# Making the keys of a first softmax bound block by block, and queueing matmul products when their operand is done

## The chip, the cores and the metric

The kernel runs on one core of a Trainium2 chip. The metric is the device time of one execution in microseconds (us). The engines of a core work side by side, each through its own queue in order: PE (TensorE, matrix products), ACT (ScalarE, activation functions), DVE (VectorE), POOL (GpSimd) and SP (SyncE, which here issues nearly all transfers). An instruction that waits for an operand holds up all that is queued behind it on its engine.

## The reference

The input x has 2048 rows of 512 numbers. The result mixes self-attention with 32 heads of 16 numbers and a gated feed-forward network:

```python
g = sigmoid((x * gate_w).sum(-1, keepdims=True))
qkv = x @ wqkv                                   # 3 x 32 heads x 16
p = softmax(einsum("bhqd,bhkd->bhqk", q, k) / 4) # 2048 x 2048 for each head
a = einsum("bhqk,bhkd->bhqd", p, v) @ wo
b = (silu(x @ w_gate) * (x @ w_up)) @ w_down     # inner width 1792
return g * a + (1 - g) * b
```

All inputs and the output are bfloat16. The exponentials of 32 x 2048 x 2048 scores are most of the work outside the matrix products.

## The kernel before, in words

**Units, tiles and pairs.** A unit is one block of 512 queries for four heads: 4 x 8 = 32 units. The first four units are the first four heads for the four query blocks. A unit has 16 key tiles of 128 keys. A tile's scores are four products of 128 keys by 512 queries, one for each head. They come as two pairs: a pair fills a tile of two PSUM banks (`s_t`), and ACT makes its exponentials in one instruction of 128x1024 (`e_t<-s_t`). For some tiles, the V tiles, DVE makes the exponentials instead: PE writes single scores (`d_t`), DVE turns each into the bits of an approximate exponential, and two or three further passes over the whole tile, of which POOL may take a strip, refine it into two or four copies (`c_t`). V tiles are taken from the end of a unit's keys, tiles for ACT from its beginning. PE then multiplies either kind of numerator by the values (`o_ps<-e_t,vaug` and `o_ps<-c_t,vaug`); a V tile needs two or four such products, an ACT tile one.

**The bound.** The softmax does not look for a row's maximum. A bound on the scores, from a weighted sum of the magnitudes of q, goes into an extra row of the q operand. For the first four heads the weights are the largest magnitudes of k over all keys. At the start only 768 rows of x (`FK`, six key tiles, `FT`) have been loaded. So the kernel first makes a provisional bound from the keys of those rows (`kneg1`) and begins with the scores of the first six tiles with a q (`q0a`) that has this bound. Meanwhile the keys of the other 1280 rows are made in three blocks of 512, 512 and 256 (`k0_pieces`): four groups of matmuls each, `kp<-xT,mt` in the profile. DVE takes a block's largest magnitudes (`largest`, `kpart<-kp`) and copies the keys to SBUF (`kaug<-kp,onescol`). When the three blocks are done, `bound_all` folds their magnitudes into `kneg0` with three `k_neg` operations (`mt<-mt,kpart`). `q0_again` then has PE add the exact bound to a fresh q (`bound_add`, in the profile `qp<-mt`); `variants` copies this to SBUF and makes its two masked forms (`mt<-qp`, `qx<-mt,vsel`). Scores from the seventh tile on read this q, and so do all V tiles of the first unit. The part of the output that came from the first six tiles is later multiplied by the ratio of the two bounds.

**The order.** The order of every engine's instructions is written out when the kernel is built, by a planner. It keeps a clock for each engine (`plan.pe`, `plan.act`, `plan.dve`, `plan.pool`; 0 is the first pair's start), emits pairs, and fills what PE has left between them with value products and pieces of side work. Side work is in chains (`Chain`): a chain has a first slot (a slot is a tile's turn), a deadline, and chains that must have been emitted (`begun`) or finished (`after`) before. `pick` takes the ready chain with the earliest deadline; a chain with a deadline below 0 goes ahead of the one in progress. So in the kernel before, the fresh q's products (released at slot 1) are left after three of four pieces for the keys (slot 2). `later` queues DVE work with a cost and the time from which it can run; `need` forces a chain out at a given slot. PSUM has three banks for side work and `d_t`; ten numerator tiles can be open (`EB`).

**The marks.** `TURNS` is a string that steers the planner: of the two characters for pair n, the first concerns PE's filling, the second DVE's and POOL's choices, and "." leaves both to the standing rules.

Of the kernel before, what the change touches and what calls it, by code (L numbers as in the profile page):

```python
# [17 lines left out]
class Chain:  # L18
# [3 lines left out]
    def __init__(self, pieces, release, deadline, after=(), gap=0, cond=None, begun=()):  # L22
        self.begun = list(begun)
        self.pieces = list(pieces)
        self.n = len(self.pieces)
        self.rest = sum(p[0] for p in self.pieces)
        self.i = 0
        self.owed = 0
        self.release = release
        self.deadline = deadline  # L30
        self.after = list(after)
        self.gap = gap
        self.cond = cond
        self.done_at = None

    def out(self):
        return self.i >= self.n
# [4 lines left out]
    def ready(self, slot):  # L42
        if slot < self.release:
            return False
        for a in self.begun:
            if a.i < a.n:
                return False
        for a in self.after:
            if a.i < a.n or a.owed or slot < a.done_at + self.gap:
                return False  # L50
        return self.cond is None or self.cond()


class Pacer:
# [30 lines left out]


TURNS = (
    "........s...................k................w....o........l......a.b.........j.k.............a."
    "b............................x...............u...........l.................................q...."
    "...........v.n...uatf..tc..f............j.......a..............ya..........w.................ti."  # L90
    ".....m..f......t...l......c...s...i..lk.........b.........s.....k....v........e..u.............."
    "...q....................k..f............hx......................................e.......d......."
    ".....t.........v..............a....d.v.........f..jn.....r.................l..............d..g.."
    "s...k........x..c.j..nc...f...........h....gc.......h..v............a....x....e........f........"
    ".....m.u.q......................ow.................lh..........n.......g........c..v.......y...."
    "...ng.i...f..f........o.....................c............w..................j....n............o."
    "......................a......d...................l....i.......ex.......y........a.h...........h."
    "....f..........t...............m............j.................f.a...a........w.............f...."
    "..................a..........l.............mcq.r.........v.............w........................"
    "..............g..........................y.r.q..a.........d.............s.o....o..o.d..o...q...."  # L100
    ".......d............................................o........d.u....bt..e...j..f..s............."
    "..............................a.................e.....................h....n...dc..............."
    ".q.f......o....gh.........o...gn....o....d................d"
)


# [1 line left out]
def kernel(  # L108
# [400 lines left out]
    def k_bound(b):  # L509
        vec.tensor_reduce(out=kb[:, b:b + 1], in_=kst[b][:, :], axis=AX.X, op=ALU.max, apply_absolute_value=True)  # L510

    def v0(p, t0, i0, i1):

        for i in range(i0, i1):
            for dc in range(DC):
                mm(p[:, 64 * i:64 * i + 64], lhsT=xT[:, dc, (t0 + i) * P:(t0 + i + 1) * P], rhs=wv[:, dc, 0:64],
                   start=(dc == 0), stop=(dc == DC - 1))
# [5 lines left out]
    def v0_pieces(t0, n):  # L523

        st = {}

        def pc(k):
            def f():
                if k == 0:
                    st["p"] = m_tile("vp")  # L530
                for i in (k,):
                    for dc in range(DC):
                        mm(st["p"][:, 64 * i:64 * i + 64], lhsT=xT[:, dc, (t0 + i) * P:(t0 + i + 1) * P],
                           rhs=wv[:, dc, 0:64], start=(dc == 0), stop=(dc == DC - 1))
                spend("F", 0.8)
                if k == n - 1:
                    later(0.6, end)
            return f

        def end():  # L540
            vec.tensor_copy(**v0_out(st["p"], t0, n))
            m_free(st["p"], plan.dve)
        return [(0.8, pc(k), k == 0, "F", None) for k in range(n)]

    def v_pieces(tt):

        def end(p):
            dst = vaug[:, tt, 4 * VC:G * 4 * VC].rearrange("p (h c) -> p h c", c=VC)[:, :, 1:1 + DH]
            vec.tensor_scalar(out=ge[:, tt:tt + 1], in0=p[:, 63:64], scalar1=-40.0, scalar2=40.0, op0=ALU.max, op1=ALU.min)
            vec.tensor_copy(out=dst, in_=p[:, 64:D].rearrange("p (h c) -> p h c", c=DH))  # L550
            m_free(p, plan.dve)
        return columns(DC, "vp", lambda dc: xT[:, dc, tt * P:(tt + 1) * P], lambda dc: wv[:, dc, 63:D],
                       lambda p: later(0.69, lambda: end(p)), c0=63)

# [49 lines left out]
    def q0_pieces(qb):  # L604
# [11 lines left out]
        def clear():  # L616
            vec.tensor_scalar(out=mt[:, 5, :].bitcast(U16), in0=mt[:, 5, :].bitcast(U16), scalar1=0x7FFF, scalar2=None,
                              op0=ALU.bitwise_and)

        def bound():  # L620
            bound_add(st["p"], kneg0, mt[:, 5, :])
            spend("C", 1)
            variants(st["p"], q0[qb], work.tile([P, QBW], BF16, tag="qst", name="qst")[:, :])
        return (columns(DC, "qp", lambda dc: wpad[0][:, dc, :], lambda dc: xT[:, dc, qb * QBW:(qb + 1) * QBW], landed),
                [(1, bound, False)])

    def bound_add(p, kn, aq):
        for j in range(4):
            mm(p[32 * j:32 * j + 32, :], lhsT=kn[:, 32 * j:32 * j + 32], rhs=aq, start=False, stop=True,
               tile_position=(0, 32 * j), skip_group_check=True)  # L630

    def variants(p, to, q, more=()):

        def copy():
            vec.tensor_copy(out=q, in_=p[:, :])
# [2 lines left out]
        def select():  # L638
            for v in range(2):
                vec.tensor_scalar(out=to[:, v, :], in0=q, scalar1=vsel[:, v:v + 1], scalar2=None, op0=ALU.mult)  # L640
        key = object()
        later(0.6, copy, key=key)
        later(0.4, select, key=key)
# [109 lines left out]
    def emit_pair(bs, ride=0):  # L753
        i = pairs[0] % 2
        plan.pe = max(plan.pe + (FLIP if plan.mode != "R" else 0.0), s_end[i])
        plan.mode = "R"
        ride = d_slots(1 - bs[0] % 4 // 2)[:ride]
        s_t = ps_s.tile([P, 2 * QBW], F32, tag="s", name="s_t")
# [311 lines left out]
    def pv(n, k=None, most=QBW):  # L1070
# [9 lines left out]
            o_of[un] = ps_o.tile([P, QBW], F32, tag="o", name="o_ps")  # L1080
        if v_of(n) is not None:
            force(v_of(n))
        o = o_of[un]
        first = pvs[un] in ((0, FT) if un == 0 else (0,))
        last = un == 0 and pvs[un] == FT - 1 or pv_left(un) == 1
# [249 lines left out]
    def k0_pieces(i, k0, w):  # L1335
        c0 = QBW - w

        def end(p):
            def evict():
                vec.tensor_scalar(out=kaug[:, 0, k0:k0 + w], in0=p[:, c0:QBW], scalar1=onescol[:, 0:1],  # L1340
                                  scalar2=None, op0=ALU.add)
                m_free(p, plan.dve)
            later(0.67 if w == QBW else 0.4, lambda: largest(i, p[:, c0:QBW]))
            later(0.6 if w == QBW else 0.35, evict)
        return columns(DC, "kp", lambda dc: wpad[1][:, dc, :], lambda dc: xT[:, dc, k0:k0 + w], end, c0)

    def bound_all():
        def f():
            k_neg(kneg0, 2, kneg1)
            for i in (3, 4):  # L1350
                k_neg(kneg0, i, kneg0)
        later(1.1, f)

    again_ps = []

    def q0_again():
# [7 lines left out]
            ratio_done.append(plan.act + 0.1)  # L1364
        p = again_ps[0]
        bound_add(p, kneg0, aq0)
        spend("C", 1)
        variants(p, q0[0], q0_bf[1])
        at.setdefault(8, []).append(lambda: later(0.6, differ))
        at.setdefault(10, []).append(scale)  # L1370

    def scale_part(p):
        def f():
# [2 lines left out]
            part_scaled.append(0)  # L1376
        later(0.6, f)

    second = [pace.add(k0_pieces(2 + i, k0, min(QBW, S - k0)), 2, -100 + 0.1 * i)
              for i, k0 in enumerate(range(FK, S, QBW))]  # L1380
    known = pace.add([(0.2, bound_all, False)], 2, -98, second)
    qp_again = pace.add(columns(DC, "qp", lambda dc: wpad[0][:, dc, :], lambda dc: xT[:, dc, 0:QBW], again_ps.append),
                        1, -101)
    again = pace.add([(1, q0_again, False)], 2, -97, [known, qp_again])
    v_next = pace.add(v0_pieces(FT, 8), 2, -96)
    v_late = pace.add(v0_pieces(FT + 8, KT - FT - 8), 2, -95, [v_next])
    parts = pace.add(columns(1, "rp", lambda k: sbc_t, lambda k: ratio, scale_part), 3, 11, [again], 1,
                     cond=lambda: part_done and ratio_done and ratio_done[0] <= plan.pe)
    need[5] = [again]
    need[8] = [v_next]  # L1390
    need[10] = [v_late]
    need[14] = [parts]
# [8 lines left out]

        return v_rest[n - QB * KT] if QB * KT <= n < QB * KT + KT else None

    def v_done(n):
        return v_of(n) is None or v_of(n).done()
    prev = []
    for qb in range(1, QB):
        d = qb * KT
        q, bd = q0_pieces(qb)
        q = pace.add(q, 0, d - 13, [known])  # L1410
        bd = pace.add(bd, 0, d - 11, [q])
        need.setdefault(d - 5, []).append(bd)
        q_of[qb] = bd
    for qb in range(QB):
# [118 lines left out]
    def pv_list(now):  # L1533
# [7 lines left out]
        r = []  # L1541
        for n in range(un * KT + done_a[un], FT if early else un * KT + hi[un]):
            bs = range(4 * n, 4 * n + 4)
            if not all(b in e_end for b in bs) or now is not None and (max(e_end[b] for b in bs) > now or not v_done(n)):
                break
            r.append(n)
        r = [(n,) for n in r]
        r = r if early else [(n, k) for ready, n, k in vready if n // KT == un and (now is None or ready <= now and v_done(n))] + r
        item = cut.get("item")
        return r if item is None else [item] + [i for i in r if i != item]  # L1550

# [304 lines left out]
```

## Time and profile before

| what | value |
|---|---|
| median of three runs | 749.05 us (747.89 to 749.58) |
| the profiled execution's own time | 747.7 us |
| its span, first to last instruction | 746.0 us |
| mean granted PE clock | 0.998 of full speed |
| PE, ACT and DVE busy | 725.8, 729.8 and 719.5 us |
| numerator pairs on ACT | 756 |
| scores evicted by DVE for V tiles | 536, four to a tile |

The profile is of one execution. Times of single instructions are from the start of its span. A row of the list of instructions has the start, the time it took, the engine and line, the operation, what it writes and reads with shapes, and how many instructions are merged in it; in brackets the idle time before it and what ended that. Line 192 is the helper through which every matmul goes, 195 that of ACT and 204 that of DVE, POOL and SP, so operations are told apart by the tiles that they write and read. A row of the table by stretch has, for each engine, busy microseconds and in brackets the number of instructions, then the granted PE clock (1.00 is full speed), the mean busy share of the 16 DMA engines (it can exceed 1 where packets overlap) and the rate in GB/s. Weight loads (PEld) run beside the matmuls.

### The profile page before, as it was taken

What the parts mean: (1) busy time and instruction counts of PE and PEld (TensorE: products, weight loads), DVE (VectorE), ACT (ScalarE), POOL (GpSimd) and SP (SyncE); (2) the same over time, 40 slices, a digit from 0 to 9 for tenths busy, and PEclk for the clock granted to TensorE, in tenths of its full rate; (3) what the DMA queues carried; (4) which work ended last, traced back from release to release, by engine and by line L of the source; (5) the groups of instructions that cost most, each with busy time, mean ns of one, the idle gap of its engine ahead of it and who ended that gap; (6) DMA issues with size and microseconds to landing.
All of it is one profiled execution on the core that took longest, in us unless ns stands there. A gap on an engine that the chain in (4) does not pass through costs nothing.

```text
span 746.0 us, 22982 instructions
## 1 busy us (share of the span) xinstructions
PE 725.8 (97%) x9246; PEld 216.3 (29%) x9247; DVE 719.5 (96%) x1249; ACT 729.8 (98%) x828; POOL 289.6 (39%) x365
## 2 busy tenths in 40 slices
PE   8899999999999999999999999999999999999997
PEld 4222222223322222222222233322222332222222
DVE  5799999999999999999999999999999999999995
ACT  6899999999999999999999999999999999999996
POOL 7114244324442332444444345643344433454220
PEclk9999999999999999999999999999999999999999
DMA  9000212244120013211100132211000232100001
GB/s 224 10 2 16 52 30 44 58 118 117 37 52 13 13 28 96 62 42 32 42 19 10 43 87 46 68 36 41 20 13 26 63 82 56 34 20 13 16 30 36
DMA packets 91283, 34.45 MB, mean 46 GB/s; under 512 B 76000, under 2 KB 90728, under 8 KB 91176
## 3 DMA queue, kind: packets, MB, share of 16 engines
q1 hardware_dynamic: 89448, 32.66, 18.2%
q8 instruction: 72, 1.18, 0.6%
q10 hardware_dynamic: 1728, 0.33, 0.2%
q14 instruction: 35, 0.29, 0.1%
HBM read 21.42 MB, written 2.35 MB: 32 GB/s over the span
## 4 chain that ended last, share of the span: by engine, by line
PE 36%; DVE 14%; ACT 13%; issue 5%; DMA 0%; SPq 0%; DVEq 0%; ACTq 0%
PE s_t L192 12%; ACT e_t L195 12%; PE o_ps L192 11%; DVE c_t L204 10%; PE ops L192 7%; PE gu L192 4%; DVE kaug L204 1%; ACT th L195 1%; DVE mt L204 1%; DVE gs L204 1%; PE qp L192 1%; DMA on<-osb 0%; DVE osb L204 0%; DVE qst L204 0%; SPq L204 0%
## 5 line engine op out<-in xcount | busy, mean ns | idle before, releaser
L195 ACT ACTIVATE e_t<-s_t 128x1024 bf16<-128x1024 f32 x756 | 706.8, 1096 | 4.2 <-PE s_t L192 3.2
L204 DVE TENSOR_SCALAR c_t<-d_t 128x512 uint16<-128x512 f32 x456 | 300.2, 685 | 6.3 <-PE d_t L192 5.8
L192 PE MATMUL s_t<-qx,kaug 32*128 32x512 bf16 (+1 forms) x1200 | 234.0, 385 | 8.8 <-ACT e_t L195 7.0
L204 POOL TENSOR_SCALAR c_t<-c_t 128x352 uint16<-128x352 uint16 (+17 forms) x169 | 121.8, 720 | 189.1 <-DVE c_t L204 116.5
L192 PEld LDWEIGHTS <-kaug 32*128 32x128 bf16 (+1 forms) x2048 | 81.9, 91 | 308.5 <-issue 304.9
L192 PE MATMUL d_t<-qx,kaug 32*128 32x512 bf16 x440 | 151.2, 384 | 0.9 <-DVE qx L204 0.9
L192 PE MATMUL o_ps<-e_t,vaug 128*32 128x512 bf16 (+2 forms) x1600 | 150.2, 374 | 0.3 <-DVE vaug L204 0.3
L192 PE MATMUL o_ps<-c_t,vaug 128*32 128x512 bf16 (+2 forms) x1408 | 125.3, 371 | 0.1
L204 DVE TENSOR_SCALAR c_t<-c_t 128x2048 uint16<-128x2048 uint16 (+3 forms) x195 | 123.1, 646 | 0.6 <-PE o_ps L192 0.3
L204 POOL TENSOR_TENSOR c_t<-c_t 128x480 bf16<-128x480 bf16 (+9 forms) x58 | 65.6, 1145 | 130.8 <-DVE c_t L204 110.6
L192 PEld LDWEIGHTS <-vaug 128*32 128x32 bf16 x3232 | 68.0, 95 | 103.5 <-issue 89.5
L192 PE MATMUL gu<-xT,wg 128*32 128x512 bf16 x896 | 71.8, 383 | 0.0
L192 PE MATMUL gu<-xT,wu 128*32 128x512 bf16 x896 | 68.3, 382 | 0.4 <-DVE c_t L204 0.4
L192 PE MATMUL ops<-wd_t,mt 128*32 128x512 bf16 x672 | 56.8, 382 | 0.0
L204 DVE TENSOR_TENSOR c_t<-c_t 128x1568 bf16<-128x1568 bf16 (+11 forms) x53 | 50.9, 960 | 0.0
L204 DVE TENSOR_SCALAR kaug<-d_t 128x512 uint16<-128x512 f32 x64 | 42.7, 685 | 0.1
L204 POOL TENSOR_SCALAR c_t<-kaug 128x352 uint16<-128x352 uint16 (+15 forms) x37 | 25.7, 694 | 35.7 <-DVE c_t L204 16.8
L195 ACT ACTIVATE th<-gu 128x512 bf16<-128x512 f32 x56 | 38.7, 690 | 0.0
L204 DVE SCALAR_TENSOR_TENSOR mt<-gs,gu 128x512 bf16<-128x512 bf16 x56 | 38.1, 681 | 0.5 <-PE gu L192 0.2
L204 DVE SCALAR_TENSOR_TENSOR gs<-th,gu 128x512 bf16<-128x512 bf16 x56 | 38.1, 681 | 0.5 <-ACT th L195 0.3
L192 PE MATMUL s_t<-q,kaug 32*128 32x512 bf16 (+1 forms) x188 | 36.6, 384 | 0.9 <-ACT e_t L195 0.5
L192 PEld LDWEIGHTS <-mt 128*32 128x32 bf16 (+1 forms) x1059 | 25.2, 95 | 30.2 <-issue 22.6
(148 smaller groups left out, 565.5 us busy)
## 6 DMA issues: line engine op xcount, KB each, us to landing
wg<-in_B_w_gate_dram SPq DMA_DIRECT2D x56, 128.0 KB
wu<-in_B_w_up_dram SPq DMA_DIRECT2D x56, 128.0 KB
on<-osb SPq DMA_DIRECT2D x120, 16.0 KB
rb<-rr SPq DMA_DIRECT2D x15, 128.0 KB
wd_t<-in_B_w_down_dram SPq DMA_DIRECT2D x7, 256.0 KB
qx<-qst SPq DMA_DIRECT2D x96, 16.0 KB
qx<-aq SPq DMA_DIRECT2D x96, 16.0 KB
out_dram<-o_t SPq DMA_DIRECT2D x12, 128.0 KB
```

The lines of the kernel that those rows point to most:

```text
L192: return ordered(nc.tensor.matmul(*args, **kw))
L195: ordered(nc.scalar.activation(*args, **kw))
L204: return lambda *a, **kw: ordered(f(*a, **kw))
```

## The change

The three key blocks are released a slot earlier, each after the one before, the first after all four pieces of the fresh q, and none before 2.3 us on the planner's clock. A block's `k_neg` now follows its `largest` at once, so `bound_all` goes away; the copy of the middle block's keys is given a later start. The exact bound's product is queued only when the planner's clock has reached the end of the last `k_neg` (`hold`), and is forced a slot later than before. The same is done for the bounds of the other three query blocks. Scores with the exact q, and value products with values that DVE has just copied, are placed no earlier than the planned end of those DVE operations (`q0_at`, `v_at`). The values of tiles 6 to 13 (`v_next`) are held until all key blocks are out. `TURNS` is replaced.

```diff
+        self.hold = None
...
-        return self.cond is None or self.cond()
+        return (self.hold is None or self.hold()) and (self.cond is None or self.cond())
...
 TURNS = (
-    "........s...................k................w....o........l......a.b.........j.k.............a."
+    "...........g.q..i..o.....r.......da..........t.................................................."
...
         def end():
             vec.tensor_copy(**v0_out(st["p"], t0, n))
             m_free(st["p"], plan.dve)
+            for i in range(n):
+                v_at[t0 + i] = plan.dve + 0.1
...
+            st["at"] = plan.dve + 0.12
 
         def bound():
             bound_add(st["p"], kneg0, mt[:, 5, :])
-            spend("C", 1)
+            spend("C", 1, st["at"])
...
         plan.pe = max(plan.pe + (FLIP if plan.mode != "R" else 0.0), s_end[i])
+        if FT <= bs[0] // 4 < KT:
+            plan.pe = max(plan.pe, q0_at[-1])
...
         if v_of(n) is not None:
             force(v_of(n))
+        plan.pe = max(plan.pe, v_at.get(n, 0.0))
...
-            later(0.67 if w == QBW else 0.4, lambda: largest(i, p[:, c0:QBW]))
-            later(0.6 if w == QBW else 0.35, evict)
+
+            def top():
+                largest(i, p[:, c0:QBW])
+                k_neg(kneg0, i, kneg1 if i == 2 else kneg0)
+                known_at.append(plan.dve)
+            later(1.03 if w == QBW else 0.76, top)
+            later(0.6 if w == QBW else 0.35, evict, plan.pe + 1.9 if i == 3 else None)
...
-    def bound_all():
-        def f():
-            k_neg(kneg0, 2, kneg1)
-            for i in (3, 4):
-                k_neg(kneg0, i, kneg0)
-        later(1.1, f)
...
         bound_add(p, kneg0, aq0)
-        spend("C", 1)
-        variants(p, q0[0], q0_bf[1])
+        spend("C", 1, known_at[-1] + 0.12)
+        variants(p, q0[0], q0_bf[1], note=q0_at)
...
-    second = [pace.add(k0_pieces(2 + i, k0, min(QBW, S - k0)), 2, -100 + 0.1 * i)
-              for i, k0 in enumerate(range(FK, S, QBW))]
-    known = pace.add([(0.2, bound_all, False)], 2, -98, second)
     qp_again = pace.add(columns(DC, "qp", lambda dc: wpad[0][:, dc, :], lambda dc: xT[:, dc, 0:QBW], again_ps.append),
                         1, -101)
-    again = pace.add([(1, q0_again, False)], 2, -97, [known, qp_again])
+    second = [pace.add(k0_pieces(2 + i, k0, min(QBW, S - k0)), 1, -100 + 0.1 * i)
+              for i, k0 in enumerate(range(FK, S, QBW))]
+    for a, c in zip([qp_again] + second, second):
+        c.hold = lambda a=a: plan.pe >= 2.3 and a.out()
+    again = pace.add([(1, q0_again, False)], 2, -97, begun=second + [qp_again])
+    again.hold = lambda: len(known_at) == len(second) and known_at[-1] <= plan.pe
     v_next = pace.add(v0_pieces(FT, 8), 2, -96)
+    v_next.hold = lambda: all(c.out() for c in second)
...
-    need[5] = [again]
+    need[6] = [again]
...
-        q, bd = q0_pieces(qb)
-        q = pace.add(q, 0, d - 13, [known])
+        q, bd, hold = q0_pieces(qb)
+        q = pace.add(q, 0, d - 13, second)
         bd = pace.add(bd, 0, d - 11, [q])
+        bd.hold = hold
```

## The prediction

> **What bounds the kernel now.** I read the engine totals first, then busy time by stretch, then the waits and single instructions of the one stretch that stands out.
>
> ```profile
> span 746.0 us, 22982 instructions
> PE 725.8 (97%) x9246; PEld 216.3 (29%) x9247; DVE 719.5 (96%) x1249; ACT 729.8 (98%) x828; POOL 289.6 (39%) x365
> ...
> L195 ACT ACTIVATE e_t<-s_t 128x1024 bf16<-128x1024 f32 x756 | 706.8, 1096 | 4.2 <-PE s_t L192 3.2
> ```
>
> Three engines are full together. 512 key tiles (32 units of 16) need a softmax numerator; 756 pairs, which is 378 tiles, get it on ScalarE (ACT), and the other 134 on VectorE (DVE; 456+64+16 evictions of d_t, four to a tile). One tile is worth 2 x 706.8/756 = 1.87 us of ACT. On DVE it costs 4 x 0.685 for evictions, 2 x 0.688 for masks and up to 1.218 for the product, 5.3 us before GpSimd takes a share. So a hole in one engine can't simply be filled by another.
>
> The busy time by stretch (columns: PE, weight loads, DVE, ACT, POOL, granted clock, DMA share, GB/s):
>
> ```profile
> 12.50:20.00 7.50, 6.82 (x88) 2.16 (x86) 3.68 (x7) 7.50 (x9) 1.80 (x3) 1.00 0.89 269
> 20.00:28.00 8.00, 6.26 (x71) 2.75 (x72) 4.04 (x9) 4.77 (x6) 0.00 (x0) 0.79 0.03 7
> ...
> 28.00:720.00 692.00, 680.52 (x8763) 198.76 (x8765) 686.01 (x1167) 691.23 (x781) 273.55 (x334) 1.00 0.18 42
> ```
>
> From 28 to 720 us ACT idles 0.77 us of 692, DVE 6.0, PE 11.5. From 20 to 28 us ACT idles 3.23 and DVE 3.96, at a clock of 0.79. The instructions of that place, PE's, then DVE's, then ACT's:
>
> ```profile
> 18.95 0.40 PE L192 MATMUL qp<-xT,mt 128*32 128x512 bf16 x4
> 20.82 0.40 PE L192 MATMUL qp<-mt 128*32 128x512 bf16 x4 [1.47 <-DVE mt L204]
> ...
> 22.67 0.37 PE L192 MATMUL d_t<-qx,kaug 32*128 32x512 bf16 x1 [0.92 <-DVE qx L204]
> ```
>
> ```profile
> 15.93 0.69 DVE L204 TENSOR_REDUCE kpart<-kp 128x1 f32<-128x512 f32 x1 [3.48 <-PE kp L192]
> ...
> 19.64 1.12 DVE L204 SCALAR_TENSOR_TENSOR mt<-mt,kpart 128x128 bf16<-128x128 bf16 x3
> ```
>
> ```profile
> 11.11 9.27 ACT L195 ACTIVATE e_t<-s_t 128x1024 bf16<-128x1024 f32 x10 [0.19 <-PE s_t L192]
> 21.86 1.02 ACT L195 ACTIVATE e_t<-s_t 128x1024 bf16<-128x1024 f32 x1 [1.47 <-PE s_t L192]
> 23.97 1.02 ACT L195 ACTIVATE e_t<-s_t 128x1024 bf16<-128x1024 f32 x1 [1.09 <-PE s_t L192]
> 25.40 1.02 ACT L195 ACTIVATE e_t<-s_t 128x1024 bf16<-128x1024 f32 x1 [0.40 <-PE s_t L192]
> 26.69 1.02 ACT L195 ACTIVATE e_t<-s_t 128x1024 bf16<-128x1024 f32 x1 [0.27 <-PE d_t L192]
> ```
>
> The product of the exact bound (20.82) stands at the head of PE's queue until DVE's three k_neg are done. The scores of pair 11, at 21.37, are behind it, so ACT runs dry. Then PE slows down:
>
> ```profile
> 22.00:23.00 1.00, 0.33 (x2) 0.03 (x2) 0.62 (x2) 0.88 (x1) 0.00 (x0) 1.00 0.00 0
> 23.00:24.00 1.00, 1.00 (x15) 0.47 (x14) 0.69 (x1) 0.03 (x1) 0.00 (x0) 0.70 0.00 0
> 24.00:25.00 1.00, 1.00 (x10) 0.34 (x6) 0.00 (x0) 1.00 (x1) 0.00 (x0) 0.50 0.00 0
> ```
>
> PE was busy 1.61 us of the 4.00 from 19 to 23; the clock then halves until about 26.6, and ACT's next three waits (1.09 + 0.40 + 0.27 = 1.76) lie there.
>
> **The change part by part.** *Keys earlier.* The release falls from slot 2 to slot 1, behind the four pieces of the new q. The planner's clock starts at the first scores (10.68 in the trace), so its 2.3 is 12.98. Before, the 16 pieces (the last four of half width) ran from 12.51 to 19.35, with two tiles' value products between them and one q piece at the very end. Two to three pieces fit between two pairs; with one value product fewer ahead I put the last key product's end at 18.2, against 18.69. No DMA, SP or POOL instruction moves with these chains. A value product put later costs nothing as long as the ten numerator buffers suffice, and the planner forces it when they run short.
>
> *One k_neg per block.* Three stay three, at 0.35 each, but two move ahead of the last block, and the last block's eviction (0.48, starting 19.25) moves behind. That takes 0.70 + 0.48 = 1.2 us off the way from the last key product to the bound, which took 2.07 (18.69 to 20.76); DVE's idle 3.48 and 0.38 us are the cover. The operand is ready at 18.2 + 0.9 = 19.1 instead of 20.76. From there to both selects took 1.8 us (20.82 to 22.62), so the exact q is there at about 21.0.
>
> *Queued when done.* PE then no longer stands in front of the product, and pairs 11 and 12, which use the old bound, go ahead. ACT made ten in 9.27, so twelve end at 11.11 + 12 x 0.927 = 22.2, and the exact scores must be ready by then: 0.9 us to spare for a product of 0.4. What is late next is DVE: two evictions (0.74 + 0.48) follow the selects, and the first d_t work starts then instead of at 23.08. If the clock also stays up, all of 1.47 + 1.76 = 3.23 us goes. The bounds: 0 if the key products meet x late, which the trace can't show exactly (no load held them at 14.34); at most 3.23 on ACT.
>
> *The clock.* The gaps of 1.47 and 0.92 us precede the fall; with value products and v pieces free to run, I take PE to be over half busy, and the clock to hold. The Trainium skill, "TensorE: Matmul & The Clock Gate", section "Why this matters for your kernels", warns only of idle gaps above about 3 us. By that rule gaps as short as these would not slow PE and removing them would not bring back the 1.76; the sum would be only 1.47. The trace shows a fall after shorter gaps; the granted clock decides, and I take 3.23.
>
> *Holds elsewhere.* From 28 us on, ACT waits for PE for 0.8 us altogether and PE for DVE for 1.2 (0.5 + 0.4 + 0.3). The holds can win at most 0.8, and can lose as much by placing a product later; I take 0. The planner's own waits issue nothing.
>
> *The table.* It reorders everything after. Its step is one tile, 1.87 us. Upward, the idle 5.1 us of DVE from 28 to 200 us (172 less 166.9) would pay for one more tile: -1.87. Downward I bound it at three tiles, +5.6, for which DVE would have to waste 16 us more. Both tables are of one kind with similar numbers of marks, and the steady stretch leaves ACT 0.77 us: I take 0.
>
> **Sum.** The profiled execution took 747.7 (span 746.0 and 1.7 around it). 747.7 - 3.23 = 744.5. It lies 1.35 below the median of the runs shown, so against 749.05 the sum is 745.8, 0.43% faster. About 0.2%, or 1.5 us, is what a measurement of this kernel can tell from no change.
>
> **The rivals.** *Half of it stays.* If the key products still have to wait for x (so that the change does not do what it says), or PE is again under half busy and its clock falls, ACT keeps a wait near 22 us. For it: DMA is still at a share of 0.85 at 13 to 14 us, and the late eviction of the last block but one keeps a bank from the v pieces. Against: 0.9 us of margin. With only the first wait gone: 749.05 - 1.47 = 747.6. By the page's rule on gaps above, if it alone held, the same 747.6 would follow.
>
> *The table gives tiles back to ACT: slower.* Place: 28 to 720 us. Each V tile that the new order fails to place costs 1.87. Three outweigh the 3.23 by more than the resolution: 749.05 - 3.23 + 5.61 = 751.4. For it: under the old marks ACT is all but without a gap in that stretch, so there is more to lose than to win, and each mark acts on a numbered pair of a planned order that all three engines must keep up with. Against: two would give 749.6, no change; only from three is it slower.
>
> *The table wins a tile.* DVE's 3.96 idle us at 20 to 28 go too, and with the 5.1 after 28 they are worth one tile: 745.82 - 1.87 = 744.0.
>
> **How the numbers follow.** Forecast (waits gone, table within a tile) 0.46, with its own range 744.5 to 747.4; half stays 0.17; tiles lost 0.23; a tile or more won 0.14. Half of the second case is beyond 0.2% (747.55), half within it; of the third I put 0.20 on three tiles or more, 0.03 on two. Faster: 0.46 + 0.14 + 0.08 = 0.68; same: 0.09 + 0.03 = 0.12; slower 0.20. The range takes in a tile and a half won (about 743.0) and goes up to the three tiles lost (751.4).
>
> **What would show it.** Right: ACT busy 8.0 of 8.0 from 20 to 28 us, no PE wait of over 0.5 us for mt, clock 1.00 throughout, first scores from qx before 22.2 instead of 24.69, key products beginning near 13.5, and 754 to 758 numerator pairs on ACT. Wrong: a PE wait before the first late key product (x late); a clock under 1.00 between 20 and 28; or 762 pairs and more, which is three tiles lost, with a steady stretch longer by 1.87 each.

## The result and the profile after

The changed kernel takes 744.88 us (744.41 to 745.17, six runs), the kernel before 748.47 us (747.77 to 749.58, six runs made beside them). The ratio is 0.995, with a 95% interval of 0.9937 to 0.9962: 3.6 us, or 0.5%, faster. The profiled execution after took 745.13 us; its span is 743.3 us. Of all runs shown below, one of the twelve with one product moved took 1186.19 us, for a reason that is not known, and the ratios leave it out.

Busy time by stretch, after; columns as before (PE, weight loads, DVE, ACT, POOL, granted clock, DMA share, GB/s):

```profile
12.50:20.00 7.50, 7.50 (x102) 2.26 (x100) 3.90 (x9) 7.50 (x9) 1.80 (x3) 1.00 0.85 262
20.00:28.00 8.00, 7.04 (x93) 3.10 (x90) 6.98 (x14) 8.00 (x10) 0.00 (x0) 1.00 0.04 9
28.00:720.00 692.00, 679.47 (x8719) 197.66 (x8716) 686.00 (x1170) 690.68 (x780) 271.63 (x323) 1.00 0.18 42
```

From 20 to 28 us ACT has no idle time left (4.77 of 8 us busy before, 8.00 now), and the clock stays at 1.00. In the long stretch ACT idles 1.32 us where it idled 0.77. The instructions of the place, after: PE, DVE, ACT.

```profile
13.82 0.39 PE L193 MATMUL kp<-xT,mt 128*32 128x512 bf16 x4
...
18.14 0.62 PE L193 MATMUL kp<-xT,mt 128*32 128x256 bf16 x16
...
19.56 0.39 PE L193 MATMUL s_t<-mt,kaug 64*128 64x512 bf16 x2
19.88 0.40 PE L193 MATMUL qp<-mt 128*32 128x512 bf16 x4
...
21.72 0.39 PE L193 MATMUL s_t<-qx,kaug 32*128 32x512 bf16 x2 [0.44 <-DVE qx L205]
```

```profile
18.81 0.42 DVE L205 TENSOR_REDUCE kpart<-kp 128x1 f32<-128x256 f32 x1
19.27 0.35 DVE L205 SCALAR_TENSOR_TENSOR mt<-mt,kpart 128x128 bf16<-128x128 bf16 x1
19.54 1.14 DVE L205 TENSOR_SCALAR kaug<-kp,onescol 128x256 bf16<-128x256 f32 x2
...
21.31 0.62 DVE L205 TENSOR_SCALAR qx<-mt,vsel 128x512 bf16<-128x512 bf16 x2
```

```profile
11.11 17.63 ACT L196 ACTIVATE e_t<-s_t 128x1024 bf16<-128x1024 f32 x19 [0.19 <-PE s_t L193]
```

ACT makes 19 pairs in one piece where it had four waits after the tenth. The exact bound's product runs at 19.88 without a wait, behind the scores of pair 11 (19.56). ACT's first scores with the exact q are at 21.72 (24.69 before).

The ledger on ACT: it is busy 729.8 us in both profiled executions, with 756 pairs in both. Its idle time goes from 16.2 (746.0 less 729.8) to 13.5 us (743.3 less 729.8): 3.23 us less between 20 and 28, 0.55 more between 28 and 720. That is the 2.7 us of the spans. The medians differ by more, 3.6 us. The reason is most likely the clock in the runs of before, which differs from run to run:

| mean granted clock of a run of before | runs | time, us |
|---|---|---|
| 1.0 | 1 | 745.86 |
| 0.998 | 12 | 747.56 to 747.78 |
| 0.995 | 6 | 749.07 to 749.28 |
| 0.993 | 19 | 749.40 to 750.14 |

These are 38 of the 41 runs of before made beside the experiments on three chips; the other three, at 0.994 and 0.996, took 747.65 to 747.88. The profiled execution of before is one at 0.998. For the six runs of before in the result no clock is on record; by their times, three are like those at 0.998 and three like those at 0.995 and 0.993. All six runs of the changed kernel are at 0.999 or 1.0.

### The profile page after: what moved, and what is told of

Its sections match the earlier page's. It is cut to its first block, busy times and chain, and to the rows that moved or that the text cites. A ratio compares the mean times of both kernels' runs of the same rounds, so it can differ in the third digit from the quotient of the medians.

```text
span 743.3 us, 22884 instructions
## 1 busy us (share of the span) xinstructions
PE 723.7 (97%) x9199; PEld 214.8 (29%) x9199; DVE 720.3 (97%) x1253; ACT 729.8 (98%) x828; POOL 288.0 (39%) x354
## 4 chain that ended last, share of the span: by engine, by line
PE 57%; ACT 24%; DVE 13%; issue 6%; ACTq 0%; DVEq 0%
ACT e_t L196 22%; PE s_t L193 19%; PE o_ps L193 16%; DVE c_t L205 8%; PE gu L193 7%; PE ops L193 4%; PE kp L193 2%; ACT th L196 2%; PE qp L193 2%; PE dps L193 2%; PE vp L193 2%; DVE kaug L205 1%; DVE mt L205 1%; DVE gs L205 1%; PE warm L193 1%
## 5 line engine op out<-in xcount | busy, mean ns | idle before, releaser
L205 POOL TENSOR_SCALAR c_t<-c_t 128x384 uint16<-128x384 uint16 (+15 forms) x158 | 115.5, 731 | 151.8 <-DVE c_t L205 119.1
L193 PE MATMUL o_ps<-e_t,vaug 128*32 128x512 bf16 (+2 forms) x1552 | 146.6, 380 | 0.0
L205 DVE TENSOR_SCALAR c_t<-c_t 128x2048 uint16<-128x2048 uint16 (+6 forms) x201 | 126.5, 640 | 0.1
L193 PEld LDWEIGHTS <-vaug 128*32 128x32 bf16 x3184 | 66.3, 95 | 103.5 <-issue 89.3
L205 DVE TENSOR_TENSOR c_t<-c_t 128x1568 bf16<-128x1568 bf16 (+14 forms) x54 | 50.5, 937 | 0.0
L205 DVE TENSOR_SCALAR kaug<-d_t 128x512 uint16<-128x512 f32 x60 | 39.7, 682 | 0.3 <-PE d_t L193 0.2
L205 POOL TENSOR_SCALAR kaug<-c_t 128x352 uint16<-128x352 uint16 (+14 forms) x35 | 26.6, 759 | 27.2 <-DVE c_t L205 19.8
L205 POOL TENSOR_SCALAR c_t<-kaug 128x1088 uint16<-128x1088 uint16 (+14 forms) x33 | 24.6, 745 | 27.3 <-DVE c_t L205 19.4
```

Source lines behind the costliest of these rows:

```text
L193: return ordered(nc.tensor.matmul(*args, **kw))
L205: return lambda *a, **kw: ordered(f(*a, **kw))
```

## The experiments

### Is it the code or the marks?

Four runs cross the two parts of the change: the old and the new code, each without marks, and each with the other's marks.

```diff
 TURNS = (
-    "........s...................k................w....o........l......a.b.........j.k.............a."
...
-)
+TURNS = ""
```

> The old code with an empty string of marks. Theory A (the gain lies in the first 28 us, and the marks only keep the rest tight): ACT idles about 3 us between 20 and 28 us as before, and the time is some us above 748.5, since a steady stretch without marks places fewer V tiles; I put it at 751 to 758. Theory B (the new marks made the gain): the same here; this run is only the foot for the next one.

> The new code with an empty string of marks, beside the old code with an empty string. Theory A: ACT idles under 0.5 us between 20 and 28 us, the clock stays at 1.00, and the time is 3.2 us below that of the old code without marks, give or take one tile (1.9 us). Theory B: the two are within 1 us of each other.

Measured: 766.74 us for the old code (ratio 1.0237, 1.0216 to 1.0258), 762.33 for the new (1.0182, 1.0161 to 1.0203). The stretch from 20 to 28 us of the old code without marks, and then of the new:

```profile
20.00:28.00 8.00, 6.59 (x71) 3.00 (x71) 4.71 (x10) 5.74 (x7) 0.49 (x1) 0.79 0.05 12
```

```profile
20.00:28.00 8.00, 7.11 (x90) 3.06 (x88) 6.97 (x13) 8.00 (x10) 0.00 (x0) 1.00 0.05 10
```

The code alone, with no marks on either side, is worth 4.4 us. At the start ACT idles 2.26 us in the one and not at all in the other, and the clock is 0.79 against 1.00: theory A holds there. Not all of the 4.4 us is the start's, though. From 28 to 720 us of the profiled executions ACT idles 7.75 us with the old code and 3.73 with the new, since without fitted marks the two orders differ there too. What I missed by far is the foot: without marks both kernels are 17 to 18 us slower than with their own.

The old code with the new marks, and the new code with new marks for ten pairs and old ones after:

```diff
 TURNS = (
-    "........s...................k................w....o........l......a.b.........j.k.............a."
...
+    "...........g.q..i..o.....r.......da..........t.................................................."
...
```

> The old code with the new marks. Theory A: the start is as before (ACT idle 2.5 to 3.5 us between 20 and 28 us), and since the marks now fall on another order the rest is no better: 748 to 754. Theory B: 745 to 746, as fast as the changed kernel.

> The new code with the new marks for the first 10 pairs and the old marks from the 11th on. Theory A: ACT idles under 0.5 us between 20 and 28 us; the rest loses something because the marks were laid for another order, by tiles of 1.87 us: 745 to 750. Theory B: nothing of the gain is left, 748.5 or more, although the start is clean.

Measured: 769.16 us (1.027, 1.0248 to 1.0292) and 768.07 us (1.0255, 1.0232 to 1.0278). The starts are as theory A has them (ACT idle 2.61 and 0.00 us from 20 to 28 us), but both times are far off my numbers: marks laid for another order are worse than none, by 2.4 and 5.7 us. From the list of groups and from the stretches of the old code with new marks:

```profile
L195 ACT ACTIVATE e_t<-s_t 128x1024 bf16<-128x1024 f32 x772 | 723.7, 1107 | 11.1 <-PE d_t L192 5.5 <-PE s_t L192 5.0
```

```profile
28.00:720.00 692.00, 671.33 (x8484) 195.93 (x8480) 656.09 (x1103) 683.98 (x772) 174.25 (x227) 0.99 0.17 41
```

ACT has 772 pairs instead of 756: eight tiles fewer went to DVE. DVE idles 36 us in the long stretch instead of 6, and POOL works 174 us there instead of 274. So a table without a fit costs what the slower rival of the prediction described, only much more: 16.9 us of exponentials and 6.4 us of ACT's idle time. So the changed code could not keep the old table; whether the new one adds anything is tested further down.

### What does the fall of the clock cost?

Zeros, added to the open output bank by 24 matmuls, fill PE's gap in the kernel before; the wait of the product stays. In the second run 16 more stand ahead of the first d_t product.

```diff
+    def filler(n):
+        for _ in range(n):
+            for j in range(4):
+                mm(o_of[0][32 * j:32 * j + 16, :], lhsT=vaug[:, 0, G * 4 * VC:], rhs=xT[:, 0, 0:QBW],
+                   start=False, stop=False, tile_position=(0, 32 * j), skip_group_check=True)
...
+        filler(6)
         bound_add(p, kneg0, aq0)
```

> The kernel before, with 24 more matmuls (zeros added to the open output bank, 1.3 us) queued on PE just ahead of the exact bound's product, where PE stood idle for 1.47 us. The wait itself stays. Theory C (the low share of busy time on PE halves the clock): the clock stays at 1.00 from 20 to 28 us. As the prediction has it, 1.76 us are won. As a closer look at the queue has it, the 1.09 us belong to the scores of pair 12 standing behind a d_t product that waits 0.92 us for the exact q, and the clock is worth only 0.40 + 0.27 and some tenths: 0.6 to 0.9 us. Rival (the fall has another cause, as by a rule on gaps of about 3 us): the clock falls all the same and nothing changes.

> As the last, with 16 more such matmuls (0.87 us) ahead of the first d_t product, where PE idled for 0.92 us. Theory C: clock 1.00 throughout; if one gap filled is enough, the same time as with the first alone; if each low stretch counts, only this one keeps the clock up. ACT still waits 1.47 and about 1 us. 0.6 to 0.9 us below the kernel before (1.76 by the prediction's split). Rival: no change.

Measured: 746.41 us (745.91 to 746.48; ratio 0.9966, 0.9954 to 0.9979) with the first gap filled and 746.44 (0.9968, 0.9955 to 0.9981) with both. Every run has a clock of 0.999 or 1.0. The stretch and ACT's instructions with the first gap filled:

```profile
20.00:28.00 8.00, 6.82 (x98) 2.87 (x90) 5.30 (x12) 5.61 (x7) 0.00 (x0) 1.00 0.03 7
```

```profile
21.68 1.02 ACT L195 ACTIVATE e_t<-s_t 128x1024 bf16<-128x1024 f32 x1 [1.47 <-PE s_t L192]
23.63 4.69 ACT L195 ACTIVATE e_t<-s_t 128x1024 bf16<-128x1024 f32 x5 [0.92 <-PE s_t L192]
```

Useless work on PE makes the kernel 2.5 us faster (0.34% of 749.26; 1.6 to 3.4 by the interval). ACT still waits 1.47 and then 0.92 us; the 0.40 and 0.27 us after that are gone. In the profiled execution of before the fall thus cost 0.84 us of ACT's waits, not 1.76: most of the 1.09 is a wait in PE's queue. Over the runs it cost more; many of them have a lower mean clock than the profiled one. Theory C holds for the cause, and one filled gap is enough. Of its sizes, 0.6 to 0.9 us fits the profiled execution alone; 1.76 lies within the interval of the win, but only by luck, since it was added up from the wrong waits.

Set beside the result, 748.47 less 746.41 is 2.1 us, and 746.41 less 744.88 is 1.5 us. As an estimate from two sets of runs, more than half of what the change wins is the clock's, and the rest is ACT's waits in PE's queue.

### Which product holds up whom?

The kernel before, with nothing changed but PE's order: first the bound's product behind the scores of pair 11, then also the first d_t product behind those of pair 12. Each emission is put off until the pair's scores are out.

```diff
+        flush_pe()
         spend("R", 1)
         flush_act()
         ready = plan.pe + 0.38
...
-        bound_add(p, kneg0, aq0)
+        late_pe.append(("bound", lambda: bound_add(p, kneg0, aq0)))
         spend("C", 1)
```

> The kernel before, with one thing moved: the exact bound's product stands behind the value product and the scores of pair 11 on PE, not ahead of them; every other engine's order and the rest of PE's are as before. Theory D (the next product in line takes the wait over): ACT's 1.47 us before pair 11 go, but pair 12 stays behind the d_t product that needs the exact q, so that ACT reaches pair 12 at the same time as before; 0.0 to 0.3 us won. Rival (the wait at the head of the queue is the cost in itself): 1.2 to 1.5 us won.

Measured: 749.14 us, ratio 1.0002 (0.999 to 1.0014). PE's waits and ACT's:

```profile
20.72 0.40 PE L192 MATMUL qp<-mt 128*32 128x512 bf16 x4 [0.91 <-DVE mt L204]
22.56 0.37 PE L192 MATMUL d_t<-qx,kaug 32*128 32x512 bf16 x1 [1.45 <-DVE qx L204]
```

```profile
24.12 1.02 ACT L195 ACTIVATE e_t<-s_t 128x1024 bf16<-128x1024 f32 x1 [2.92 <-PE s_t L192]
```

Theory D holds: pair 11 runs on time, and the whole wait, 2.92 us, comes one pair later, behind the next product that needs the exact q. Removing one wait at the head of the queue wins nothing while another of the same origin follows.

> As the last, and the first d_t product stands behind the scores of pair 12. So both products that need the exact q are out of the way of the pairs that don't, while the keys are as late as before. Theory D: pairs 11 and 12 run on time; pair 13 needs the exact q, which is there at 22.6, and ACT waits there for 1 to 2 us; 1.0 to 1.8 us won, and the rest of the change's 3.2 us needs the earlier keys. Rival (the earlier keys are of no use, the order on PE is all): 3 us won.

Measured: 748.02 us, ratio 0.9974 (0.9957 to 0.999), in two groups: five runs at a clock of 0.999 or 1.0 with 745.06 to 745.22 us, seven at 0.992 to 0.995 with 747.88 to 749.54. The profiled execution is one of the second group. Its stretches:

```profile
22.00:23.00 1.00, 0.74 (x5) 0.11 (x4) 0.33 (x2) 0.60 (x1) 0.00 (x0) 0.61 0.00 0
23.00:24.00 1.00, 1.00 (x10) 0.34 (x6) 0.57 (x1) 0.00 (x0) 0.00 (x0) 0.50 0.00 0
...
28.00:29.00 1.00, 1.00 (x11) 0.14 (x8) 0.78 (x3) 0.63 (x1) 0.00 (x0) 0.50 0.00 0
29.00:30.00 1.00, 1.00 (x14) 0.21 (x10) 1.00 (x2) 0.76 (x2) 0.00 (x0) 0.98 0.00 0
```

By the ratio the win is 2 us (1.2 by the medians), about what I had with 1.0 to 1.8; the split says more. Where the clock holds, order alone reaches 745.1. Where it falls, more than half of the win is lost. Theory D had pair 12 on time, and it was not: in the profiled execution ACT waited 0.68 us for it and then 1.76 for pair 13.

To see whether the clock is all that sets the two groups apart, the same order with zeros ahead of the two products that wait:

```diff
-            late_pe.append(("d", lambda: score(d_t[:, :], 4 * n + i, rows)))
+            late_pe.append(("d", lambda: (filler(3), score(d_t[:, :], 4 * n + i, rows))))
...
-        late_pe.append(("bound", lambda: bound_add(p, kneg0, aq0)))
+        late_pe.append(("bound", lambda: (filler(4), bound_add(p, kneg0, aq0))))
```

> The kernel before, with both products that need the exact q behind pairs 11 and 12 as in the run of that kind, and with 28 zero matmuls (1.5 us) in front of the two. Theory F (that run was as fast as the changed kernel whenever its clock stayed up, so the late keys cost little but the clock): clock 0.999 or 1.0 in every run and 745.0 to 745.5 us, with a spread under 1 us. Rival (its fast runs had another cause): a spread of 3 us or more as in that run.

Measured: 745.18 us (745.04 to 746.04), ratio 0.9957 (0.9942 to 0.9972), every run at 0.999 or 1.0. ACT's waits in it:

```profile
21.33 1.02 ACT L195 ACTIVATE e_t<-s_t 128x1024 bf16<-128x1024 f32 x1 [0.68 <-PE s_t L192]
23.36 4.69 ACT L195 ACTIVATE e_t<-s_t 128x1024 bf16<-128x1024 f32 x5 [1.01 <-PE s_t L192]
```

Theory F holds, though two runs in five, at 745.85 and 746.04, lie above my range. Two waits of ACT remain, 0.68 and 1.01 us: pair 12 stands behind the bound's product, and pair 13 needs the exact q. So the rival of the run before was near the truth where the clock holds: with the keys as late as before, order on PE, together with the zeros, comes within 0.3 us of the changed kernel's 744.88. What the earlier bound brings beside that is mostly that the clock holds without zeros, in all six runs of the changed kernel against five of twelve.

### Does the hold matter once the keys are early?

```diff
                 known_at.append(plan.dve)
+                if i == 4:
+                    bound_add(again_ps[0], kneg0, aq0)
...
-        bound_add(p, kneg0, aq0)
         spend("C", 1, known_at[-1] + 0.12)
```

> The changed kernel, with only the exact bound's product put back to where it stands in line as soon as the last k_neg is written out: ahead of two value products, the scores of pair 11 and all that follows; marks and everything else as in the changed kernel. Theory E (with the keys early, the product waits so little that its place hardly matters): PE waits 0.4 to 0.7 us for it, ACT loses 0 to 0.3 us, the clock stays up; within 0.5 us of the changed kernel, that is 0.4 to 0.5% below the kernel before. Rival (the hold is what wins): ACT loses 1.5 us or the clock falls, and half the gain or more is gone.

Measured: 745.28 us (744.77 to 745.48), ratio 0.9953 (0.9938 to 0.9968). PE's wait, and ACT's:

```profile
19.41 0.40 PE L193 MATMUL qp<-mt 128*32 128x512 bf16 x4 [0.60 <-DVE mt L205]
```

```profile
20.67 8.36 ACT L196 ACTIVATE e_t<-s_t 128x1024 bf16<-128x1024 f32 x9 [0.56 <-PE s_t L193]
```

Theory E holds in the main: by the medians the hold of this product is worth 0.4 us of the 3.6, less than the 0.2% that can be told from no change, and the two sets of runs overlap. ACT lost 0.56 us, more than my 0.3: pair 11's scores stand behind the product and two value products. This takes away the product's place alone; the planned waits for the pairs and for d_t stayed.

### When is x there?

```diff
-    for a, c in zip([qp_again] + second, second):
-        c.hold = lambda a=a: plan.pe >= 2.3 and a.out()
+    for a, c in zip(second, second[1:] + [qp_again]):
+        c.hold = lambda a=a: a.out()
```

> The changed kernel with the key blocks released ahead of the fresh q and without the planner's 2.3 us, to see when x is there; the marks no longer fit, so only the start is read. If x is late, as one rival of the prediction had it, PE's first key products (queued at 12.5 us) wait until 13.5 us or more, and ACT starves. If x is early: no wait, products from 12.5 us on. My estimate is a wait until 12.8 to 13.3.

PE's first key products:

```profile
12.50 0.39 PE L193 MATMUL s_t<-mt,kaug 64*128 64x512 bf16 x2 [0.42 <-ACT e_t L196]
12.82 0.83 PE L193 MATMUL kp<-xT,mt 128*32 128x512 bf16 x12
```

They follow the third pair's scores without a wait, and the products of the other two blocks do not wait either. x is there by 12.8 us, at the early end of my estimate or before it, and a full microsecond before the changed kernel uses it at 13.82. The rival in which x comes late is out. (The time, 766.63 us, is that of marks that don't fit.)

### The new start by hand, with the old marks

The kernel before with its own marks, and with its order after 28 us as it was. One `k_neg` follows each block's maximum, the evictions of the last two blocks come after the last `k_neg`, the bound's product goes behind pair 11's scores and the first d_t behind pair 13's. The keys' products stay where they were.

```diff
+        flush_pe(None if bs[0] // 4 >= FT else "bound")
         spend("R", 1)
...
-            later(0.67 if w == QBW else 0.4, lambda: largest(i, p[:, c0:QBW]))
+            def top():
+                largest(i, p[:, c0:QBW])
+                k_neg(kneg0, i, kneg1 if i == 2 else kneg0)
+            later(0.67 if w == QBW else 0.4, top)
...
-            k_neg(kneg0, 2, kneg1)
-            for i in (3, 4):
-                k_neg(kneg0, i, kneg0)
```

> The kernel before with its own marks and its order after 28 us untouched, but the change's start put in by hand: one k_neg per block on DVE right after the block's maximum, both evictions of the last two blocks after the last k_neg, the exact bound's product behind pair 11's scores, and the first d_t behind pair 13's. The operand is ready 1.1 us earlier than before, the exact q at about 22.0, and pair 13 loses 0.2 to 0.6 us. Theory G (the gain is the 3.2 us of the start, and the old marks held the rest as well as the new ones or better): clock 1.00, ACT idle under 0.8 us between 20 and 28 us, 743.5 to 744.8, at or below the changed kernel's 744.9. Rival (the new marks brought part of the gain): 745.5 or more.

Measured: 744.22 us (743.57 to 744.23, five runs), ratio 0.9938 (0.9924 to 0.9953). The stretches:

```profile
20.00:28.00 8.00, 7.69 (x99) 3.00 (x97) 7.26 (x14) 7.93 (x10) 1.44 (x2) 1.00 0.04 10
...
28.00:720.00 692.00, 680.56 (x8776) 198.85 (x8774) 686.04 (x1166) 691.23 (x781) 272.94 (x335) 1.00 0.18 43
```

ACT idles 0.07 us at the start and 0.77 in the long stretch, as much there as in the kernel before; pair 13 lost none of the 0.2 to 0.6 us that I gave it. This version is 0.7 us below the changed kernel, every one of its runs below every one of those; that is under the 0.2% that I set as the bound, from another set of runs, and the two intervals overlap. What it does settle is theory G: the old marks with the new start give the whole gain, so the gain needs none of the new marks. It needs no key product moved forward either.

## Why the prediction was right

**The place and the mechanism.** The bound's product and a d_t product at the head of PE's queue, ACT running dry behind them, PE falling to half its clock: all three were there, and all of the 3.23 us between 20 and 28 us went. The run with one product moved shows the queue, those with zeros show the clock. The range, 743.0 to 751.4, took in no change and a loss as well, so that the time alone proves little.

**Keys earlier: wrong, and without consequence.** I had the last key product end at 18.2. It ended at 18.76 (18.14 and 0.62), against 18.69 before: the blocks began 0.5 us sooner, but the fourth q piece now goes ahead of them. The version by hand, with the key products where they were, does as well.

**One k_neg per block: right.** From the last key product's end to the operand it took 0.86 us (18.76 to 19.62, which is 19.27 and 0.35) instead of 2.07: the 1.2 us of the forecast. Since the keys came no earlier, the operand was ready 1.1 us before its old time, not the 1.7 that the forecast of 19.1 means.

**The exact q at 21.0: too early.** It came at 21.93. Half a microsecond of that is the operand. The product then starts 0.26 us after it, behind pair 11's scores, and the evictions that I put behind the selects (1.14 us) run ahead of the copy, so that from the product to both selects it takes 2.05 us and not 1.8. So the 0.9 us to spare shrank to some 0.1: the first exact scores waited 0.44 us for it and were still in time for ACT.

**The clock: right in kind, wrong in size twice.** Of ACT's waits in the profiled execution I gave it 1.76 us; the run with zeros leaves it 0.84. Against that I carried the 1.35 us between the profiled execution and the median along as if the change could not touch it. That difference is most likely the fall of the clock itself, since at 0.995 the kernel before took some 1.5 us longer than at 0.998, and at 0.993 some 2 (table above); in the changed kernel it is gone.

**The table: right by luck.** Zero was right, with 756 pairs as before. But I bounded a bad table at three tiles and 5.6 us, and one that doesn't fit costs eight tiles and some 20 us. The stretch after 28 us lost 0.55 us of ACT; whether through the table or through the holds elsewhere, both of which the forecast put at nothing, no run separates.

**The sum.** For the profiled execution 744.5 was forecast and 745.13 came: 3.23 at the start, less the 0.55, less small parts. Against the median 745.8 was forecast and 744.88 came: the 1.35 outweighed that. The number is close because two errors of opposite sign met.

## What to carry to other kernels

A wait at the head of an in-order queue is worth removing only together with the next one of the same origin; list what in the queue needs the late operand, and put all of it behind the work that doesn't. Price a stall on PE not only by its length but by what the granted clock does after it, and look at the clock of several runs, since one profiled execution may show the mild case. Where an order is tuned by marks on numbered steps, any change ahead of them must carry a new fit or leave the later order alone, as the version by hand did.

## What the runs showed of the hardware that I had not expected

The clock fell without any long gap on PE. The stretch ahead of the fall in the kernel before, in the one with both products moved, and, where the clock held, in the kernel before with zeros in its first gap:

```profile
19.00:23.00 4.00, 1.61 (x18) 0.30 (x17) 3.00 (x9) 2.41 (x3) 0.00 (x0) 1.00 0.11 30
...
18.80:22.20 3.40, 1.76 (x24) 0.70 (x17) 2.79 (x8) 2.72 (x4) 0.00 (x0) 1.00 0.15 36
...
19.00:23.00 4.00, 2.91 (x46) 0.93 (x39) 2.93 (x9) 2.24 (x3) 0.00 (x0) 1.00 0.12 30
```

PE was busy 1.61 of 4.00 us in the first, with no idle piece above 1.47, 1.76 of 3.40 in the second, and 2.91 of 4.00 in the third. So to be over half busy, which the prediction took for enough, is not: 1.76 of 3.40 is 52%. Nor does the order alone decide, since the second kept its clock in five runs of twelve. Matmuls that add zeros were enough to keep it up. The Trainium skill ("TensorE: Matmul & The Clock Gate", section "Why this matters for your kernels") asks, against drops of throughput, for no idle gaps on PE above about 3 us. The first two had none there, and the clock fell all the same.

The half clock comes in pieces of one length. The end of the fall in the kernel before:

```profile
25.00:26.00 1.00, 1.00 (x17) 0.69 (x15) 0.00 (x0) 0.60 (x1) 0.00 (x0) 0.50 0.00 0
26.00:27.00 1.00, 1.00 (x15) 0.51 (x14) 0.34 (x1) 0.73 (x2) 0.00 (x0) 0.59 0.08 16
```

From the stretches of 1 us, it lasted 0.6 + 1 + 1 + 0.82 = 3.42 us in the profiled execution of before (a share of 0.70 in the first microsecond, 0.59 in the last), and 0.78 + 6 + 0.04 = 6.82 us with the two products moved. The old code with the new marks shows a third size: a clock of 0.50 from 21.74 to 31.98, which is 10.24 us or three times 3.41, with PE busy throughout. The pieces also keep to one beat. The two falls in the trace of the old code without marks begin at 23.29 and 170.06 (read from stretches of 0.1 us), those of the old code with the new marks at 21.74 and 130.97; the distances, 146.77 and 109.23 us, are 43.0 and 32.0 times 3.413. The Trainium skill, on the same page ("TensorE: Matmul & The Clock Gate"), section "What's actually happening", gives a free-running window of 3413 ns. The traces agree with it in the length of the pieces and in the beat.

An estimate from this: each piece takes 0.5 x 3.41/746 = 0.0023 off the mean clock of a run, so that 0.998, 0.995 and 0.993 would be one, two and three of them. Only the first was traced in the kernel before, and the three runs at 0.994 and 0.996 fit no whole number. By the table above the first piece costs the kernel before some 1.8 us (from a single run at 1.0), the second 1.5, the third 0.6. How many of them a run gets differs from run to run of one program. That it depends on where the window stands when the gap comes would fit, and was not tried.
